# Keys multiplied in place, and K and V loaded in 48 KB runs instead of 24 KB

## The chip, the cores and the metric

One core of one Trainium2 chip. The metric is the device time of one execution in microseconds (us). The kernel before takes 186.91 us (median of 4 runs, 186.84 to 186.94). All comparisons use runs that were recorded as fast; where a run was recorded as slow, it is named and left out. The profiled span is about 1.3 us shorter than the device time. A load of K or V fetches one contiguous run for each of 128 partitions. In the traces each run is one packet, so a load gives each of the 16 DMA engines 8 packets, and each engine reports separately when its part has landed. "First engine" below is the one that reports first.

## The reference, cut to what matters

One decode step of a transformer block for two sequences (B = 2): a modulated layer norm, attention of one query over the last 1,024 keys of 32 heads with 192 numbers each, and a gated feed-forward part. All tensors are bf16.

```python
q = (h @ wq).reshape(B, 1, 32, 192).transpose(0, 2, 1, 3)
k = k_cache[:, :, Sk - 1024:, :]            # B x 32 x 1024 x 192
v = v_cache[:, :, Sk - 1024:, :]
p = softmax(einsum('bhqd,bhkd->bhqk', q, k) * 192 ** -0.5)
o = einsum('bhqk,bhkd->bhqd', p, v) ... @ wo
```

K and V of both sequences are 50 MB of the 76.9 MB that are read. A score needs one multiplication for each number of K, so there is little work for each byte.

## The kernel before

A partition holds one head and a quarter of its positions: 128 partitions are 32 heads x 4 quarters, and each has 256 positions j. A quarter is contiguous in memory, 96 KB for each partition. An arena of six slots of 24 KB for each partition holds weights and tiles of 64 positions of K or V.

```python
TT = 64                        # positions in a tile
SLOT = TT * Dh                 # 12,288 bf16 = 24 KB
NS = 6
tiles = [("k", 0, t) for t in range(NTL)] + [("v", 0, 0)]
for t in range(NTL):
    tiles += [("k", 1, t)] + ([("v", 0, t + 1)] if t + 1 < NTL else [])
tiles += [("v", 1, t) for t in range(NTL)]
for n, it in enumerate(tiles):
    place[it] = ((n + NS - 1) % NS * SLOT, SLOT)
...
def pump(*consumed):           # issue loads, in order, as far as their slots are free
    queue["done"].update(consumed)
    while queue["next"] < len(items):
        it = items[queue["next"]]
        if not all(x in queue["done"] for x in items[:n] if overlap(x, it)):
            break
        S.dma("sp", k_dma(view(it), source(it)), sem_of[it], writes=keys(it), ...)
...
```

The scores of 16 positions are made in three steps. DVE multiplies keys and q into one of four product buffers (`d_mul`). PE adds 192 products down to 32 by six matmuls with the identity (`p_reduce`). DVE sums the rest for two such groups at once (`c_sum`).

```python
def d_mul(b, t, c):
    pz = c % 4
    lo = c % CPT * JC * Dh
    S.op("dve", tensor_tensor(out=prod[:, pz, :, :], in0=view(("k", b, t), lo, ...), in1=qbc[:, b, :]..., op=mult),
         reads=keys(("k", b, t), lo, JC * Dh) + [("qbc", b)], writes=[("prod", pz)])
def p_reduce(b, c):
    ...  # six matmuls: lhsT=ident_b, rhs=prod[:, pz, :, t * GC:(t + 1) * GC]
         # reads=[("prod", pz), "ident_b"], writes=[bank(pz)]
```

After a sequence's last keys comes the softmax. For each 64 positions of V, DVE then makes a masked copy of the weights (`Em`), and PE multiplies it with V (32 matmuls, "PV"). All loads of K, V and weights are issued by SP on one queue, in the order of `items`.

## Time and profile before

The page, as far as the argument needs it. The first three lines are 40 equal slices of the span: busy tenths of DVE, the granted clock of PE, and the busy share of the 16 DMA engines. Below are the load queue's line, the chain that ended last, three groups of instructions (busy us, mean ns | idle before, and what ended it) and the K and V loads with the time from issue to landing.

```profile
DVE  6114000048697696975593999999965856002311
PEclk9999999997988999879559999999998589995597
DMA  9989999999999999999999999999999999999991
...
q1 hardware_dynamic: 4188, 76.88, 97.3%
...
DVE 41%; DMA 35%; PE 21%; SPq 1%; issue 1%; ACT 1%
...
L510 PE MATMUL ps<-prod,ident_b 128*128 128x512 bf16 x192 | 50.7, 410 | 25.1 <-DVE prod L498 24.8
L498 DVE TENSOR_TENSOR prod<-arena,qbc 128x3072 bf16<-128x3072 bf16 x32 | 54.7, 1750 | 2.7 <-DMA arena<-in_A_k_cache_dram 2.7
...
L517 DVE TENSOR_REDUCE S_sb<-ps 128x32 f32<-128x1024 f32 x16 | 19.5, 1221 | 14.4 <-PE ps L510 14.4
...
arena<-in_A_k_cache_dram SPq DMA_DIRECT2D x8, 3072.0 KB, 32.1
arena<-in_A_v_cache_dram SPq DMA_DIRECT2D x8, 3072.0 KB, 23.8
```

The DMA row stands at 9 from the second slice to the last but one, with a single 8, and the queue is busy 97.3% of the span. DVE is busy 57%. So the loads bound the kernel. The chain says "DVE 41%", and this has to be read with care: the chain goes back from the last load through its issue to the computation that freed its slot, although that load then stood in the queue behind others for most of its time. A K load takes 32.1 us to land and occupies the engines only 7.3 us.

The end of the chain, in order of time (start, us, what), shows the tail. The load in its first line is the last but one of w_down; the last lands at 182.78 us, while PE is at work on what came before:

```profile
156.96 25.44 DMA arena<-in_B_w_down_dram
182.40 0.04 issue
182.44 0.65 PE ps L661 x16
...
183.12 0.34 DVE fin L666
```

### The profile page before, as it was taken

To read this page: it belongs to the slowest core of one execution; us is meant where nothing else is said; L and a number is where in the kernel's file an instruction comes from. 1 tells how busy PE (TensorE), PEld (TensorE's weight loads), DVE (VectorE), ACT (ScalarE), POOL (GpSimd) and SP (SyncE) were. 2 spreads that over 40 slices of the span, in tenths; PEclk is the share of its full clock that TensorE was granted. 3 is DMA by queue.
4 is the path that set the end of the run, shared out by engine and by line. 5 is a ranking of instruction groups with operands and counts; after the bars stand their busy time and mean duration, and the time that the engine had idled before them with its cause. 6 is when DMAs were issued, how large, how long until landed. Compare 5 with 4: busy or idle time off the path is not lost.

```text
span 185.6 us, 2065 instructions
## 1 busy us (share of the span) xinstructions
PE 105.1 (57%) x923; PEld 48.5 (26%) x923; DVE 105.1 (57%) x98; ACT 14.2 (8%) x26; POOL 6.4 (3%) x23
## 2 busy tenths in 40 slices
PE   0015720838638375473299496886962599416572
PEld 0011200223213121121253242423311366315321
DVE  6114000048697696975593999999965856002311
ACT  2022100060000000000100000000101000200610
POOL 8500000000000000000000000000000000000000
PEclk9999999997988999879559999999998589995597
DMA  9989999999999999999999999999999999999991
GB/s 331 440 375 450 461 433 403 434 434 424 424 434 424 434 445 434 422 429 429 426 434 424 424 440 422 424 445 440 429 429 429 441 418 456 398 404 421 408 390 38
DMA packets 4213, 77.01 MB, mean 415 GB/s; under 512 B 491, under 2 KB 621, under 8 KB 1261
## 3 DMA queue, kind: packets, MB, share of 16 engines
q1 hardware_dynamic: 4188, 76.88, 97.3%
q8 instruction: 7, 0.11, 0.2%
q14 instruction: 2, 0.01, 0.0%
q10 hardware_dynamic: 16, 0.01, 0.0%
HBM read 76.88 MB, written 0.00 MB: 414 GB/s over the span
## 4 chain that ended last, share of the span: by engine, by line
DVE 41%; DMA 35%; PE 21%; SPq 1%; issue 1%; ACT 1%
DVE prod L498 23%; DMA arena<-in_A_k_cache_dram 21%; DMA arena<-in_B_w_down_dram 14%; PE ps L510 11%; DVE S_sb L517 10%; PE ps L561 8%; DVE Em L547 6%; SPq L282 1%; DVE negm L527 1%; ACT E_sb L535 1%; PE ps L538 1%; PE ps L531 1%; DVE M L523 0%; PE ps L661 0%; PE ps L525 0%
## 5 line engine op out<-in xcount | busy, mean ns | idle before, releaser
L510 PE MATMUL ps<-prod,ident_b 128*128 128x512 bf16 x192 | 50.7, 410 | 25.1 <-DVE prod L498 24.8
L498 DVE TENSOR_TENSOR prod<-arena,qbc 128x3072 bf16<-128x3072 bf16 x32 | 54.7, 1750 | 2.7 <-DMA arena<-in_A_k_cache_dram 2.7
L510 PEld LDWEIGHTS ps<-prod,ident_b 128*128 128x128 bf16 x192 | 17.8, 104 | 57.4 <-DVE prod L498 37.5
L561 PE MATMUL ps<-arena,Em 128*64 128x384 bf16 x256 | 26.1, 369 | 7.1 <-DVE Em L547 7.1
L517 DVE TENSOR_REDUCE S_sb<-ps 128x32 f32<-128x1024 f32 x16 | 19.5, 1221 | 14.4 <-PE ps L510 14.4
L561 PEld LDWEIGHTS ps<-arena,Em 128*64 128x64 bf16 x256 | 15.7, 124 | 17.0 <-DVE Em L547 9.1
L547 DVE TENSOR_TENSOR Em<-E_sb,maskE 128x2048 bf16<-128x2048 bf16 x8 | 18.2, 2283 | 2.8 <-PE ps L561 2.8
L472 PE MATMUL ps<-arena,hT 128*2 128x512 bf16 x60 | 6.6, 615 | 10.0 <-DMA arena<-in_A_wq_dram 9.0
L482 DVE CAST qrow<-ps 128x512 bf16<-128x512 f32 x1 | 0.7, 692 | 15.7 <-PE ps L472 15.7
L611 PE MATMUL ps<-arena,oT 128*17 128x160 bf16 x192 | 5.0, 276 | 6.2 <-DMA arena<-in_A_wo_dram 6.2
L618 DVE TENSOR_TENSOR lnt<-ps,modR 128x160 f32<-128x160 f32 x1 | 0.3, 325 | 14.1 <-PE ps L611 14.1
L611 PEld LDWEIGHTS ps<-arena,oT 128*17 128x17 bf16 x192 | 4.4, 109 | 6.5 <-DMA arena<-in_A_wo_dram 6.5
L472 PEld LDWEIGHTS ps<-arena,hT 128*2 128x2 bf16 x60 | 1.7, 114 | 14.9 <-DMA arena<-in_A_wq_dram 10.0
L568 ACT ACTIVATE On<-ps,rden 128x384 bf16<-128x384 f32 x2 | 1.2, 581 | 57.0 <-PE ps L561 57.0
L535 ACT ACTIVATE E_sb<-S_sb,nbias 128x256 bf16<-128x256 f32 x2 | 1.0, 507 | 57.9 <-DVE nbias L533 57.9
L391 PE MATMUL ps<-ident_b,crow 2*128 2x2 bf16 x5 | 0.4, 177 | 8.2 <-DMA crow<-in_c_dram 8.2
L404 PE MATMUL ps<-st,selstat 128*128 128x2 f32 x4 | 1.1, 350 | 6.1 <-ACT sqj L400 6.1
L450 PE MATMUL ps<-arena,scT 128*17 128x480 bf16 x40 | 4.3, 596 | 0.3 <-DMA arena<-in_w_mod_dram 0.3
L396 DVE CAST X<-xr 128x160 f32<-128x160 bf16 x1 | 0.2, 244 | 7.4 <-DMA xr<-in_A_x_dram 7.4
L632 PE MATMUL ps<-arena,h2T 128*2 128x384 bf16 x40 | 3.8, 484 | 0.6 <-DMA arena<-in_B_w_up_dram 0.3
L641 DVE TENSOR_TENSOR aR<-ps,gl 128x384 bf16<-128x384 f32 x1 | 0.6, 557 | 4.3 <-PE ps L632 4.3
L458 DVE TENSOR_SCALAR opc<-modR 128x160 f32<-128x160 f32 x2 | 0.5, 244 | 4.3 <-ACT modR L455 4.3
(79 smaller groups left out, 49.1 us busy)
## 6 DMA issues: line engine op xcount, KB each, us to landing
arena<-in_A_k_cache_dram SPq DMA_DIRECT2D x8, 3072.0 KB, 32.1
arena<-in_A_v_cache_dram SPq DMA_DIRECT2D x8, 3072.0 KB, 23.8
arena<-in_w_mod_dram SPq DMA_DIRECT2D x1, 4800.0 KB, 14.1
arena<-in_A_wq_dram SPq DMA_DIRECT2D x1, 4608.0 KB, 32.0
arena<-in_A_wo_dram SPq DMA_DIRECT2D x1, 4480.0 KB, 28.3
arena<-in_A_wq_dram SPq DMA_DIRECT2D x1, 3072.0 KB, 20.6
arena<-in_A_wo_dram SPq DMA_DIRECT2D x1, 2720.0 KB, 17.2
arena<-in_B_w_gate_dram SPq DMA_DIRECT2D x1, 1920.0 KB, 20.4
```

Source lines behind the costliest of these rows:

```text
L282: return lambda e: e.dma_start(dst, src)
L450: last = e.matmul(ps[32 * i:32 * i + RM, half, 0:MH].rearrange("p (m n) -> p m n", n=DR), lhsT=scT[:, k, :], rhs=wv[:, 3 * half:3 * half + ...
L472: last = e.matmul(ps[32 * i:32 * i + B, n, :], lhsT=hT[:, k, :], rhs=wv[:, kk, i, n * QW:(n + 1) * QW], start=(k == 0), stop=(k == KT - 1) ...
L498: S.op("dve", lambda e: e.tensor_tensor(out=prod[:, pz, :, :], in0=view(("k", b, t), lo, JC * Dh).rearrange("p (j d) -> p j d", d=Dh), in1 ...
L510: last = e.matmul(o_ap, lhsT=ident_b[:, :], rhs=prod[:, pz, :, t * GC:(t + 1) * GC], start=(t == 0), stop=(t == NCH - 1))
L517: S.op("dve", lambda e: e.tensor_reduce(out=S_sb[:, b, 2 * JC * pair:2 * JC * (pair + 1)], in_=ps[:, 2 * z:2 * z + 2, :].rearrange("p k (j ...
L527: S.op("dve", lambda e: e.tensor_reduce(out=negm[:, b, :].rearrange("p (h x) -> p h x", x=XQ), in_=ps[0:1, BK_T, 0:P].rearrange("p (h x) - ...
L535: S.op("act", lambda e: e.activation(out=E_sb[:, b, :], in_=S_sb[:, b, :], func=ACTF.Exp, scale=SCALE, bias=nbias[:, b:b + 1], accum_out=d ...
L547: S.op("dve", lambda e, z=z, j0=j0: e.tensor_tensor(out=Em[:, z, :, :], in0=E_sb[:, b, j0:j0 + JE].unsqueeze(2).broadcast_to([P, JE, H]), ...
L561: last = e.matmul(ps[64 * i:64 * i + 2 * H, BK_O, 0:ON], lhsT=Em[:, z, 2 * jp:2 * jp + 2, :].rearrange("p j h -> p (j h)"), rhs=view(("v", ...
L611: last = e.matmul(ps[32 * i:32 * i + RM, BK_M, 0:DR], lhsT=oT[:, t, :], rhs=wv[:, tl, i, :], start=(t == 0), stop=(t == NT - 1), tile_posi ...
L632: last = e.matmul(ps[32 * i:32 * i + B, bk, 0:FT].rearrange("p (m r) -> p m r", r=FR), lhsT=h2T[:, k, :], rhs=wk[:, i, :, :], start=(k == ...
```

## The change

The intent is to have the same bytes moved in fewer, longer packets. The products go into the keys' own place, so the four product buffers (24 KB for each partition) become a seventh slot. K and V are loaded in tiles of 128 positions, a run of 48 KB for each partition, except sequence 0's first two K tiles. A K slot now comes free when PE has reduced the products, not when DVE has multiplied. Sums are no longer flushed at the end of each K tile, only where V follows.

```diff
-    NS = 6
+    NS = 7
...
+    K_SPLIT = [[(0, 64), (64, 64), (128, 128)], [(0, 128), (128, 128)]]
+    V_SPLIT = [[(0, 128), (128, 128)], [(0, 128), (128, 128)]]
...
-        for n, it in enumerate(tiles):
-            place[it] = ((n + NS - 1) % NS * SLOT, SLOT)
+        tiles = [("k", 0, 0, 5), ("k", 0, 1, 6), ("k", 0, 2, 0), ("v", 0, 0, 2), ("k", 1, 0, 4), ("v", 0, 1, 0), ("k", 1, 1, 2), ("v", 1, 0, 4), ("v", 1, 1, 0)]
+        for kind, b, t, z in tiles:
+            j0, n = (K_SPLIT if kind == "k" else V_SPLIT)[b][t]
+            place[(kind, b, t)] = (z * SLOT, n * Dh)
...
-        prod = sb("prod", [P, 4, JC, Dh], BF16)
...
-            S.op("dve", lambda e: e.tensor_tensor(out=prod[:, pz, :, :], in0=view(("k", b, t), lo, JC * Dh)..., op=ALU.mult),
-                 reads=keys(("k", b, t), lo, JC * Dh) + [("qbc", b)], writes=[("prod", pz)], ...)
+            S.op("dve", lambda e: e.tensor_tensor(out=kt, in0=kt, in1=qbc[:, b, :]..., op=ALU.mult),
+                 reads=[("qbc", b)], writes=keys(it, lo, JC * Dh), ...)
...
-                    last = e.matmul(o_ap, lhsT=ident_b[:, :], rhs=prod[:, pz, :, t * GC:(t + 1) * GC], ...)
+                    last = e.matmul(o_ap, lhsT=ident_b[:, :], rhs=kt[:, :, t * GC:(t + 1) * GC], ...)
...
-            c_sum(b, (t + 1) * CPT // 2 - 1)
+            if nxt[0] == "v":
+                c_sum(b, (j0 + w) // JC // 2 - 1)
```

The weights' places follow (w_o in slots 2, 3 and 6, the feed-forward weights in slots 4 and 5). The order of the items is as before except for the larger tiles.

More of the change, by code (lines that the diff above doesn't have):

```diff
@@ L161, in bass_adaLN_cond__sliding_block_cached__geglu_ffn__decode_kernel @@
     ON = 2 * Dh
-    TT = 64
     JE = 64
-    NTL = J // TT
-    CPT = TT // JC
-    SLOT = TT * Dh
+    SLOT = JE * Dh
     UNIT = 128
-    assert NTL * TT == J and CPT % 2 == 0 and TT % JE == 0
+    K_SPLIT = [[(0, 64), (64, 64), (128, 128)], [(0, 128), (128, 128)]]
+    V_SPLIT = [[(0, 128), (128, 128)], [(0, 128), (128, 128)]]
+    assert all(sum(n for _, n in x) == J and all(n % JE == 0 for _, n in x) for x in K_SPLIT + V_SPLIT)
     WQ_SPLIT = [(0, 2), (2, 3)]
@@ L194, in bass_adaLN_cond__sliding_block_cached__geglu_ffn__decode_kernel @@
         place = {("wm", 0): (0, KT * 6 * D), ("wq", 0): (2 * SLOT, wq_n[0]), ("wq", 1): (2 * SLOT + wq_n[0], wq_n[1])}
-        tiles = [("k", 0, t) for t in range(NTL)] + [("v", 0, 0)]
-        for t in range(NTL):
-            tiles += [("k", 1, t)] + ([("v", 0, t + 1)] if t + 1 < NTL else [])
-        tiles += [("v", 1, t) for t in range(NTL)]
-        for n, it in enumerate(tiles):
-            place[it] = ((n + NS - 1) % NS * SLOT, SLOT)
-        for i, (t0, _) in enumerate(WO_SPLIT):
-            place[("wo", i)] = (3 * SLOT + t0 * D, wo_n[i])
-        o_g, o_u = 0, KT * F
+        tiles = [("k", 0, 0, 5), ("k", 0, 1, 6), ("k", 0, 2, 0), ("v", 0, 0, 2), ("k", 1, 0, 4), ("v", 0, 1, 0), ("k", 1, 1, 2), ("v", 1, 0, 4), ("v", 1, 1, 0)]
+        span = {}
+        for kind, b, t, z in tiles:
+            j0, n = (K_SPLIT if kind == "k" else V_SPLIT)[b][t]
+            place[(kind, b, t)] = (z * SLOT, n * Dh)
+            span[(kind, b, t)] = (j0, n)
+        tiles = [it[:3] for it in tiles]
+        place[("wo", 0)] = (2 * SLOT, wo_n[0])
+        place[("wo", 1)] = (6 * SLOT, wo_n[1])
+        place[("wo", 2)] = (2 * SLOT + wo_n[0], wo_n[2])
+        o_g = 4 * SLOT
+        o_u = o_g + KT * F
         o_d = o_u + KT * F
@@ L209, in bass_adaLN_cond__sliding_block_cached__geglu_ffn__decode_kernel @@
             place[("wd", i)] = (o_d + r0 * D, nr * D)
-        assert len(tiles) == 16 and wq_n[0] + wq_n[1] <= 3 * SLOT
         assert all(o % UNIT == 0 and n % UNIT == 0 and o + n <= NAR for o, n in place.values())
@@ L320, in source @@
                 return B_w_down.rearrange("(p r) n -> p (r n)", r=FC)[:, r0 * D:(r0 + nr) * D]
-            _, b, t = it
+            b, (j0, n) = it[1], span[it]
             src = A_k_cache if kind == "k" else A_v_cache
-            return src[b][:, K0:Sk, :].rearrange("h (x j) d -> h x j d", x=XQ)[:, :, t * TT:(t + 1) * TT, :].rearrange("h x j d -> h x (j d)")
+            return src[b][:, K0:Sk, :].rearrange("h (x j) d -> h x j d", x=XQ)[:, :, j0:j0 + n, :].rearrange("h x j d -> h x (j d)")
         def pump(*consumed):
@@ L493, in bass_adaLN_cond__sliding_block_cached__geglu_ffn__decode_kernel, with d_mul, p_reduce @@
                  reads=[bank(BK_T + b)], writes=[("qbc", b)], name="q2_evac%d" % b)
-        def d_mul(b, t, c):
-            pz = c % 4
-            lo = c % CPT * JC * Dh
-            S.op("dve", lambda e: e.tensor_tensor(out=prod[:, pz, :, :],
-                                                  in0=view(("k", b, t), lo, JC * Dh).rearrange("p (j d) -> p j d", d=Dh),
-                                                  in1=qbc[:, b, :].unsqueeze(1).broadcast_to([P, JC, Dh]), op=ALU.mult),
-                 reads=keys(("k", b, t), lo, JC * Dh) + [("qbc", b)], writes=[("prod", pz)], name="mul%d_%d" % (b, c))
-        def p_reduce(b, c):
-            pz = c % 4
+        def d_mul(it, c):
+            b, lo = it[1], (c * JC - span[it][0]) * Dh
+            kt = view(it, lo, JC * Dh).rearrange("p (j d) -> p j d", d=Dh)
+            S.op("dve", lambda e: e.tensor_tensor(out=kt, in0=kt, in1=qbc[:, b, :].unsqueeze(1).broadcast_to([P, JC, Dh]), op=ALU.mult),
+                 reads=[("qbc", b)], writes=keys(it, lo, JC * Dh), name="mul%d_%d" % (b, c))
+        def p_reduce(it, c):
+            b, lo = it[1], (c * JC - span[it][0]) * Dh
+            pz = c % 4
+            kt = view(it, lo, JC * Dh).rearrange("p (j d) -> p j d", d=Dh)
             def f(e):
@@ L509, in f @@
                 for t in range(NCH):
-                    last = e.matmul(o_ap, lhsT=ident_b[:, :], rhs=prod[:, pz, :, t * GC:(t + 1) * GC],
+                    last = e.matmul(o_ap, lhsT=ident_b[:, :], rhs=kt[:, :, t * GC:(t + 1) * GC],
                                     start=(t == 0), stop=(t == NCH - 1))
                 return last
-            S.op("pe", f, reads=[("prod", pz), "ident_b"], writes=[bank(pz)], name="red%d_%d" % (b, c))
+            S.op("pe", f, reads=keys(it, lo, JC * Dh) + ["ident_b"], writes=[bank(pz)], name="red%d_%d" % (b, c))
         def c_sum(b, pair):
@@ L541, in softmax, with weights_v, p_pv, f @@
                  reads=[bank(BK_T)], writes=[("rden", b)], name="rec_%d" % b)
-        def weights_v(b, t):
-            for s in range(TT // JE):
-                z = (t * (TT // JE) + s) % 2
-                j0 = t * TT + s * JE
-                S.op("dve", lambda e, z=z, j0=j0: e.tensor_tensor(out=Em[:, z, :, :], in0=E_sb[:, b, j0:j0 + JE].unsqueeze(2).broadcast_to([P, JE, H]),
-                                                                  in1=maskE[:, :].unsqueeze(1).broadcast_to([P, JE, H]), op=ALU.mult),
-                     reads=[("E", b), "maskE"], writes=[("Em", z)], name="Em%d_%d" % (b, j0))
-        def p_pv(b, t):
-            for s in range(TT // JE):
-                z = (t * (TT // JE) + s) % 2
-                j0 = t * TT + s * JE
-                lo = s * JE * Dh
-                def f(e, z=z, j0=j0, lo=lo):
+        def weights_v(it):
+            b, (j0, n) = it[1], span[it]
+            for j in range(j0, j0 + n, JE):
+                z = j // JE % 2
+                S.op("dve", lambda e, z=z, j=j: e.tensor_tensor(out=Em[:, z, :, :], in0=E_sb[:, b, j:j + JE].unsqueeze(2).broadcast_to([P, JE, H]),
+                                                                in1=maskE[:, :].unsqueeze(1).broadcast_to([P, JE, H]), op=ALU.mult),
+                     reads=[("E", b), "maskE"], writes=[("Em", z)], name="Em%d_%d" % (b, j))
+        def p_pv(it):
+            b, (j0, n) = it[1], span[it]
+            for j in range(j0, j0 + n, JE):
+                z = j // JE % 2
+                lo = (j - j0) * Dh
+                def f(e, z=z, j=j, lo=lo):
                     last = None
@@ L562, in f @@
                                         lhsT=Em[:, z, 2 * jp:2 * jp + 2, :].rearrange("p j h -> p (j h)"),
-                                        rhs=view(("v", b, t), lo + 2 * jp * Dh, ON),
-                                        start=(j0 == 0 and jp < 2), stop=(j0 == J - JE and jp >= JE // 2 - 2), tile_position=(0, 64 * i))
-                    return last
-                S.op("pe", f, reads=[("Em", z)] + keys(("v", b, t), lo, JE * Dh), writes=[bank(BK_O)], name="PV%d_%d" % (b, j0))
-            if t == NTL - 1:
+                                        rhs=view(it, lo + 2 * jp * Dh, ON),
@@ L568, in p_pv @@
+                                        start=(j == 0 and jp < 2), stop=(j == J - JE and jp >= JE // 2 - 2), tile_position=(0, 64 * i))
+                    return last
+                S.op("pe", f, reads=[("Em", z)] + keys(it, lo, JE * Dh), writes=[bank(BK_O)], name="PV%d_%d" % (b, j))
+            if j0 + n == J:
                 S.op("act", lambda e: e.activation(out=On[:, b, :], in_=ps[:, BK_O, 0:ON], func=ACTF.Identity, scale=rden[:, b:b + 1]),
                      reads=[bank(BK_O), ("rden", b)], writes=[("On", b)], name="On_%d" % b)
-        for n, (kind, b, t) in enumerate(tiles):
+        made = set()
@@ L572, in bass_adaLN_cond__sliding_block_cached__geglu_ffn__decode_kernel @@
+        for n, it in enumerate(tiles):
+            kind, b, t = it
             nxt = tiles[n + 1] if n + 1 < len(tiles) else None
             if kind == "v":
-                if n == 0 or tiles[n - 1][0] == "v" or (b, t) == (tiles[n - 1][1], 0):
-                    weights_v(b, t)
-                p_pv(b, t)
-                pump((kind, b, t))
+                if it not in made:
+                    weights_v(it)
+                p_pv(it)
+                pump(it)
                 continue
-            for c in range(t * CPT, (t + 1) * CPT):
-                d_mul(b, t, c)
-                p_reduce(b, c)
-                if c % 2 == 0 and c > t * CPT:
-                    c_sum(b, c // 2 - 1)
@@ L584, in bass_adaLN_cond__sliding_block_cached__geglu_ffn__decode_kernel @@
-            pump((kind, b, t))
-            if nxt and nxt[0] == "v" and nxt[1] != b:
-                weights_v(nxt[1], nxt[2])
-            c_sum(b, (t + 1) * CPT // 2 - 1)
-            if t == NTL - 1:
+            j0, w = span[it]
+            last = j0 + w == J
+            for c in range(j0 // JC, (j0 + w) // JC):
+                d_mul(it, c)
+                p_reduce(it, c)
+                if c % 2 == 0 and c > 0 and ("S", b, c // 2 - 1) not in made:
+                    c_sum(b, c // 2 - 1)
@@ L589, in bass_adaLN_cond__sliding_block_cached__geglu_ffn__decode_kernel @@
+            pump(it)
+            if nxt[0] == "v" and nxt[1] != b:
+                weights_v(nxt)
+                made.add(nxt)
+            if nxt[0] == "v":
+                c_sum(b, (j0 + w) // JC // 2 - 1)
+                made.add(("S", b, (j0 + w) // JC // 2 - 1))
+            if last:
                 softmax(b)
```

## The prediction

> What bounds the kernel now. Data transfer, from end to end. The page gives the loads' queue 97.3% of sixteen engines' span, and the slices of DMA share stay at nine tenths from the second to the last. The windows view gives a DMA share of 0.99 to 1.02 in every 12 us stretch from 38 to 172 us. The 24 KB K tiles take 32.1 us from issue to landing, though one occupies the engines only 7.3 us, so some four are always queued. The chain of waits starts on a K load and ends on the last w_down load (landing 182.4 us), then 0.65 us PE, two 0.3 us DVE steps and the store.
>
> What the change does to the transfers. The bytes are the same. Packet records: a 24,576 B packet takes 914 ns (median), a 36,864 B one 1,364, a 38,400 B one 1,420. That is 0.0366 ns per byte plus about 14 ns per packet. A 49,152 B packet should then take about 1,814 ns (estimate), against 1,828 for two of 24 KB. Seven pairs of tiles become 48 KB runs: per engine 7 x 8 = 56 packets fewer, 56 x 14 = 0.78 us, and seven 9 ns semaphore writes fewer: 0.85 us in all, all on the bounding resource. The Trainium skill, "DMA: Bandwidth & Descriptors", section "Why small descriptors are slow", gives a fixed overhead per packet; the trace agrees, and shows it is nearly spent at 24 KB.
>
> What it does to the engines. The multiply (1.68 us, 32 of them) writes over its input; I expect the same time. Four product buffers go, and the sums are no longer flushed at each K tile's end, where DVE waited about 1.5 us for PE (at 49.7 and 61.4 us). All of this is off the critical path.
>
> The risk. A K slot comes free only after PE's reduction, not after the multiply, and frees come in 48 KB lumps. Stepping the new order with the trace's durations (multiply 1.68, sum 1.15, Em 2.2, reduction 1.48, PV block 2.8, softmax 3.8 us; 1.3 us from free to first byte), the slot is free before the queue runs dry by roughly: V0 second half 5 to 6 us, K1 second half 1.5 to 8, V1 first half -0.5 to 6, V1 second half 8 to 14, first w_o 6 to 7. Before, the worst such margin was 2 us. The low ends are PE at half clock in the first PV (5.33 us a block, as at 92.7 us). "TensorE: Matmul & The Clock Gate", Part 1, says the clock halves after an idle window of about 3.4 us; the trace agrees (half clock after the softmax, 88.0 to 98.3 us). PV now ends at about 158 to 163 us, still before the last w_o lands at 168.
>
> Sum: 186.9 - 0.85 = 186.05 without a stall; about one chance in four of a stall of 0.5 to 2 us. Predicted 186.2 us, 185.5 to 187.5.
>
> Faster by over 2%: 0.01. Within 2%: 0.96. Slower: 0.03.
>
> What shows each step: 49,152 B packets near 1,814 ns; no dip in DMA share near 104 or 118 us; last load landing near 181.9 us; multiplies still 1.68 us; fewer DVE waits on PE before 85 us; V1's first load issued before about 117 us.
>
> What would make it wrong: 48 KB packets slower per byte; in-place multiplies slower; half clock during K1 emptying the queue; a stall at V1's first load.

## More of the kernel before

SP's issues in time (start, us to the end of the last of the row) show how far ahead loads are issued:

```profile
83.89 0.54 SPq L282 DMA_DIRECT2D arena<-in_A_k_cache_dram  x1
98.07 0.54 SPq L282 DMA_DIRECT2D arena<-in_A_v_cache_dram  x1
103.81 0.54 SPq L282 DMA_DIRECT2D arena<-in_A_k_cache_dram  x1
108.87 17.75 SPq L282 DMA_DIRECT2D arena<-in_A_v_cache_dram  x4
```

The load at 98.07 us is the last quarter of V of sequence 0. The load in front of it lands at 104.68 us on the DMA engine that is done first, so this issue, the tightest of the K and V stage, is 6.6 us ahead.

## The result, and the profile after

| | before | after |
|---|---|---|
| device time, median of 4 runs | 186.91 us | 186.29 us |
| range | 186.84 to 186.94 | 186.01 to 186.47 |
| data packets of the load queue, each engine | 232.5 | 176.5 |
| last wq load lands to last V load lands, first DMA engine | 116.87 us | 116.35 us |
| last w_down load landed | 182.78 us | 182.12 us |
| multiply, mean | 1,750 ns | 1,749 ns |

The ratio is 0.9966, 95% interval 0.9949 to 0.9983: 0.3% less time, clear of noise, and well inside 2%. A ratio here and below is the mean time of one kernel's fast runs over that of the other's fast runs of the same rounds, so it is not quite the ratio of the medians. Executions over 1.5% slower than the fastest of the same kernel are left out of the means.

The lines of the page after that answer to those shown of before:

```profile
DVE  6113000039994589965994999287995658102311
PEclk9999995559999759997599999987999569996576
DMA  9989999999898989999898989999898999899991
...
q1 hardware_dynamic: 3180, 76.88, 97.2%
...
DMA 57%; DVE 22%; PE 17%; ACT 1%; issue 1%; SPq 1%
...
L510 PE MATMUL ps<-arena,ident_b 128*128 128x512 bf16 x192 | 50.0, 404 | 29.2 <-DVE arena L498 29.2
L498 DVE TENSOR_TENSOR arena<-arena,qbc 128x3072 bf16<-128x3072 bf16 x32 | 54.7, 1749 | 11.5 <-DMA arena<-in_A_k_cache_dram 11.5
...
L517 DVE TENSOR_REDUCE S_sb<-ps 128x32 f32<-128x1024 f32 x16 | 19.5, 1218 | 7.5 <-PE ps L510 7.5
...
arena<-in_A_v_cache_dram SPq DMA_DIRECT2D x4, 6144.0 KB, 27.1
arena<-in_A_k_cache_dram SPq DMA_DIRECT2D x3, 6144.0 KB, 41.5
```

The queue has 1,008 packets fewer: 896 of data (56 for each engine) and 112 of the 4 bytes by which a load reports its end. The 8s in the DMA row are no gaps: the row books a packet where it starts, and packets now last as long as 0.4 of a slice. Counted packet by packet, all 16 engines were at work in every 4 us from 16 to 176 us, before and after.

DVE's wait for PE's reductions fell from 14.4 to 7.5 us, as the unflushed sums promise. In its place DVE waits 8.8 us longer for keys. That is the cost of large tiles, which can be used only when all of them have landed. Neither matters for the time, for the loads are the bound. The chain says so too: its DVE share halves and the time moves by a third of a percent.

The tail is nearly the same: 0.74 us of PE (0.65 before) from the landing of the last load but one, two DVE steps and the store. The last load lands at 182.12 us.

```profile
155.92 25.81 DMA arena<-in_B_w_down_dram
181.73 0.04 issue
181.78 0.74 PE ps L668 x16
...
182.54 0.34 DVE fin L673
```

SP's issues after, and so the lead of the tightest one:

```profile
82.83 0.54 SPq L282 DMA_DIRECT2D arena<-in_A_v_cache_dram  x1
96.75 0.54 SPq L282 DMA_DIRECT2D arena<-in_A_k_cache_dram  x1
112.83 6.66 SPq L282 DMA_DIRECT2D arena<-in_A_v_cache_dram  x2
136.02 2.00 SPq L282 DMA_DIRECT2D arena<-in_A_wo_dram  x3
```

The first load at 112.83 us is V's first half of sequence 1. The load in front of it lands at 118.81 us on the first engine, so it is issued 6.0 us ahead, against 6.6 for the tightest one before.

The packet records of the trace (these are counts and medians over the records of the two profiled runs, not lines of a view):

```
packet      before                 after
24,576 B    2,176 of 914 ns        384 of 912 ns
49,152 B    -                      896 of 1,820 ns (mean 1,821)
35,840 B    128 of 1,329 ns        128 of 1,329 ns
```

### The profile page after: what moved, and what is told of

Its sections match the earlier page's. It is cut to its first block, busy times and chain, and to the rows that moved or that the text cites. A ratio compares the mean times of both kernels' runs of the same rounds, so it can differ in the third digit from the quotient of the medians.

```text
span 185.0 us, 2053 instructions
## 1 busy us (share of the span) xinstructions
PE 103.4 (56%) x923; PEld 47.5 (26%) x923; DVE 104.9 (57%) x98; ACT 14.2 (8%) x26; POOL 6.4 (3%) x23
## 4 chain that ended last, share of the span: by engine, by line
DMA 57%; DVE 22%; PE 17%; ACT 1%; issue 1%; SPq 1%
DMA arena<-in_A_k_cache_dram 36%; DMA arena<-in_B_w_down_dram 14%; DVE arena L498 12%; DMA arena<-in_w_mod_dram 8%; PE ps L561 7%; DVE S_sb L517 6%; PE ps L510 5%; DVE Em L547 2%; PE ps L450 2%; DVE negm L527 1%; ACT E_sb L535 1%; SPq L282 1%; PE ps L538 1%; DVE M L523 0%; PE ps L531 0%
## 5 line engine op out<-in xcount | busy, mean ns | idle before, releaser
L510 PE MATMUL ps<-arena,ident_b 128*128 128x512 bf16 x192 | 50.0, 404 | 29.2 <-DVE arena L498 29.2
L498 DVE TENSOR_TENSOR arena<-arena,qbc 128x3072 bf16<-128x3072 bf16 x32 | 54.7, 1749 | 11.5 <-DMA arena<-in_A_k_cache_dram 11.5
L510 PEld LDWEIGHTS ps<-arena,ident_b 128*128 128x128 bf16 x192 | 17.3, 102 | 61.5 <-DVE arena L498 42.9
L561 PE MATMUL ps<-arena,Em 128*64 128x384 bf16 x256 | 24.4, 356 | 5.6 <-DVE Em L547 5.6
L618 PE MATMUL ps<-arena,oT 128*17 128x160 bf16 x192 | 4.2, 250 | 4.0 <-DMA arena<-in_A_wo_dram 3.2
L618 PEld LDWEIGHTS ps<-arena,oT 128*17 128x17 bf16 x192 | 3.7, 97 | 4.3 <-DMA arena<-in_A_wo_dram 3.4
L488 PE MATMUL ps<-qrow,selq 128*128 128x192 bf16 x16 | 2.7, 364 | 1.2 <-ACT qrow L479 1.2
```

The lines of the kernel that those rows point to most:

```text
L488: last = e.matmul(ps[:, BK_T + b, 0:Dh], lhsT=selq[:, b, u * P:(u + 1) * P], rhs=qrow[:, u * Dh:(u + 1) * Dh], start=(u == 0), stop=(u == ...
L498: S.op("dve", lambda e: e.tensor_tensor(out=kt, in0=kt, in1=qbc[:, b, :].unsqueeze(1).broadcast_to([P, JC, Dh]), op=ALU.mult), reads=[("qb ...
L510: last = e.matmul(o_ap, lhsT=ident_b[:, :], rhs=kt[:, :, t * GC:(t + 1) * GC], start=(t == 0), stop=(t == NCH - 1))
L561: last = e.matmul(ps[64 * i:64 * i + 2 * H, BK_O, 0:ON], lhsT=Em[:, z, 2 * jp:2 * jp + 2, :].rearrange("p j h -> p (j h)"), rhs=view(it, l ...
L618: last = e.matmul(ps[32 * i:32 * i + RM, BK_M, 0:DR], lhsT=oT[:, t, :], rhs=wv[:, tl, i, :], start=(t == 0), stop=(t == NT - 1), tile_posi ...
```

## The experiments

The theory: the kernel is bound by its loads, every packet costs a DMA engine some 10 ns beyond its bytes, and the gain is the 56 packets fewer. The edits are shown shortened. The rivals: the gain comes from the engines (in-place products, fewer waits, other slots), or from fewer loads and completions, or is chance.

### The changed kernel again

No edit. 5 rounds, on the same chip and in the same rounds as the next three.

> Control: the changed kernel as it is. Theory (fewer, longer packets in a load-bound kernel): again 186.0 to 186.5 us, 0.3 to 0.4% under the kernel before. Rival (a chance difference of the four runs): no clear difference from 186.9.

Measured: 186.41 us (186.29 to 186.59), ratio 0.9974, interval 0.9961 to 0.9986. The gain is not chance. Its interval overlaps that of the first four runs, so the two sizes are not told apart.

### The same slots, but two loads of 24 KB for each run

```diff
-    queue["ops"][it] = S.dma("sp", k_dma(view(it), source(it)), sem_of[it], writes=keys(it), ...)
+    for lo, w in pieces(it):        # K and V in pieces of PIECE = 12288 elements
+        queue["ops"][it] = S.dma("sp", k_dma(view(it, lo, w), source(it)[..., lo:lo + w]), sem_of[(it, lo)], writes=keys(it, lo, w), ...)
```

> The changed kernel, slots, order and in-place products kept, but each 48 KB run is fetched by two loads of 24 KB. Packet theory: the gain is lost. 56 packet pairs per engine cost 11 ns more each (two of 916 ns against one of 1,821 ns), 0.62 us, and seven semaphore packets of 9 ns: 186.9 to 187.0 us, last w_down load landing about 182.8 us. Rival (the gain comes from the engines: in-place products, fewer waits of DVE for PE, the new slots): stays at 186.3.

Measured: 186.91 us (186.88 to 187.03), ratio 1.0002, interval 0.9989 to 1.0014. The whole gain is gone, with seven slots, in-place products and the new order still there. Last load landed at 182.82 us (before: 182.78). The stage from the last wq load to the last V load takes 116.88 us on the first engine, as before (116.87).

### Pieces of 12 KB

The same edit with `PIECE = 6144`.

> As a24, with pieces of 12 KB: a second dose. Packet theory: a 12,288 B packet, by a straight line between 9,216 B (350 ns) and 15,360 B (578 ns), takes about 464 ns; four take 1,858 against 1,821: 56 x 37 ns = 2.1 us, 0.3 us more for the two 24 KB tiles of K0, 0.2 us of semaphore packets. About 188.9 us, 188.3 to 189.5. Rival (engines): 186.3.

Measured: 188.23 us (188.03 to 188.40), ratio 1.0069, interval 1.0057 to 1.0082. Direction as the theory says, size below my range. The packets took 464 ns as estimated, but the stage took 118.17 us, only 1.30 us more than with 24 KB, for 128 packets more on each engine: 10.1 ns for each. From 48 to 24 KB it was 0.52 us for 56: 9.3 ns. Both include the completions. Two doses at nearly the same price fit a fixed cost for each packet; that longer runs are read better for another reason is not excluded. The estimate failed because I added up the durations of packet records, and records of neighbouring packets of one engine overlap by a few ns. The 0.2 us for completions did not show either. The distance from landing to landing is what counts: 7.305 us for eight packets of 24 KB (913.1 ns each, although a record says 916 on average), 14.535 us for eight of 48 KB (1,816.9 ns, record 1,821), and 3.69 us for eight of 12 KB (462 ns, record 464).

### The kernel before with products in place, nothing else

```diff
-            S.op("dve", lambda e: e.tensor_tensor(out=prod[:, pz, :, :], in0=view(("k", b, t), lo, JC * Dh)..., ...),
-                 reads=keys(("k", b, t), lo, JC * Dh) + [("qbc", b)], writes=[("prod", pz)], ...)
+            S.op("dve", lambda e: e.tensor_tensor(out=kt, in0=kt, ...),
+                 reads=[("qbc", b)], writes=keys(("k", b, t), lo, JC * Dh), ...)
```

> The kernel before, with only the products written over the keys (six slots and 24 KB loads kept; a K slot comes free after PE's reduction, about 1.5 us later). Packet theory: 186.9 us as before, multiplies still 1.75 us. Rival (in-place products bring the gain): 186.3. If in-place products cost something: multiplies longer than 1.75 us.

Measured: 186.96 us (186.79 to 187.09), ratio 1.0001, interval 0.9988 to 1.0015. In-place products neither cost nor gain anything by themselves; the multiplies' line:

```profile
L497 DVE TENSOR_TENSOR arena<-arena,qbc 128x3072 bf16<-128x3072 bf16 x32 | 54.7, 1749 | 2.6 <-DMA arena<-in_A_k_cache_dram 2.6
```

### As many packets, twice the loads

Each 48 KB tile is fetched by two loads of every second partition. The packets stay at 48 KB; loads and completions double.

```diff
+    for g in (0, 1):
+        S.dma("sp", k_dma(view(it)[g:P:2, :], source(it)[:, g:XQ:2, :]), sem_of[(it, g)], writes=keys(it, halves=(g,)), ...)
```

> The changed kernel with each 48 KB run tile fetched by two loads of 64 partitions each (every second partition): twice the loads and completions of those tiles, but as many packets, still of 48 KB. Packet theory: 186.4 us, at most 0.1 us more (seven more loads, 9 ns a semaphore packet), 49,152 B packets still near 1,820 ns. Rival (the number of loads and their completions is what counts, not the packets): 186.9 us, as with two 24 KB loads. Open: if 64 partitions are served worse by the engines, the packets would be longer and the run says nothing.

Measured: 186.44 us (186.32 to 186.55), ratio 0.9969, interval 0.9956 to 0.9982. The page shows that it did what it should. It has 112 packets more than the changed kernel, all of them 4-byte completions (seven loads x 16 engines), and still the stage took 116.35 us.

```profile
q1 hardware_dynamic: 3292, 76.88, 97.1%
...
arena<-in_A_k_cache_dram SPq DMA_DIRECT2D x8, 3072.0 KB, 36.8
```

So the number of loads is not it. The number of packets is, or, what these runs cannot separate from it, their length.

### How near is an empty queue? Extra DVE work

After sequence 0's softmax, DVE makes the first `Em` again, once or four times (EXTRA is 1 or 4). The result stays right.

```diff
-            for j in range(j0, j0 + n, JE):
+            for j in [j0] * (EXTRA if it == ("v", 0, 0) else 0) + list(range(j0, j0 + n, JE)):
```

> The changed kernel with one Em step (2.28 us of DVE) done twice after batch 0's softmax. Theory (engines off the critical path; in the trace V1's first half is issued at 112.8 us, about 1.3 us before its first byte can move, and the queue runs dry at about 118.3: 4.2 us of margin, 5.7 at K1's second half): no change, 186.4 us, within 0.2. Rival (DVE time counts): 188.7 us.

Measured: 186.36 us (186.26 to 186.42), ratio 0.9965, interval 0.9953 to 0.9977. 2.3 us of DVE work in the middle of the kernel cost nothing.

> The same step done four more times, 9.1 us of DVE. Theory: the margin of 4.2 us before V1's first half is used up and 4 to 6 us of empty queue appear there (K1's second half late by 9.1 - 5.7 = 3.4 us first): 190 to 192 us, with a dip of the DMA share between 103 and 125 us. Rival A (all DVE time counts): 195.5 us. Rival B (slots have nothing to do with it): 186.4 us.

Measured: 192.28 us (191.64 to 193.33), ratio 1.0288, interval 1.0261 to 1.0314. Of 9.1 us, some 5.9 reach the time. The windows (busy us of each engine, then PE clock, DMA share, GB/s) show the two gaps that the theory asked for:

```profile
90.00:100.00 10.00, 0.57 (x4) 0.37 (x6) 9.86 (x6) 0.00 (x0) 0.00 (x0) 0.50 0.94 408
100.00:110.00 10.00, 10.00 (x79) 5.57 (x76) 7.42 (x5) 0.00 (x0) 0.00 (x0) 0.86 0.61 241
110.00:120.00 10.00, 6.29 (x26) 2.02 (x24) 10.00 (x8) 0.00 (x0) 0.00 (x0) 1.00 1.09 472
120.00:130.00 10.00, 8.23 (x77) 4.65 (x78) 10.00 (x7) 0.58 (x1) 0.00 (x0) 1.00 0.84 331
```

```profile
106.46 0.54 SPq L282 DMA_DIRECT2D arena<-in_A_k_cache_dram  x1
122.54 6.66 SPq L282 DMA_DIRECT2D arena<-in_A_v_cache_dram  x2
```

The load before the one at 106.46 had landed at 104.38 us. The first new packet starts 1.3 us after the issue began, and the first packet then takes 2,284 to 2,660 ns on 14 of the engines (1,832 and 2,095 on the two that start last) instead of 1,820. The landing that follows is 18.73 us after the one before, not 14.53: 4.20 us lost. The second gap costs 1.61 us (16.14 us between landings). Together they make 5.8 us.

### The same extra work in the kernel before

The same edit on the kernel before, four times.

> The kernel before with the same Em step done four more times after batch 0's softmax (9.1 us of DVE). Theory: its margin is as thin as that of the changed one: V0's last quarter was issued at 98.1 us, its packets start at 104.2, and a load must be issued some 3 us ahead; so 9.1 - 3.1 = about 5 to 6 us of loss in ONE gap, for slots then come free every 7 us: 191.5 to 192.8 us. The changed kernel lost 5.9 us in two gaps. Rival (the change made the schedule more fragile than it was): under 190 us here.

Measured: 188.72 and 189.75 us in the two fast runs; two more, 192.04 and 193.41, were recorded as slow and are left out. Ratio 1.0124, interval 1.0095 to 1.0153. On these two runs the verdict goes to the rival: the kernel before loses 2.3 us (their mean, against 186.9) where the changed one loses 5.9. But the two runs left out are called slow for their time alone; their granted clocks (0.879 and 0.889) lie within those of the other two (0.875 and 0.900). With all four the loss would be 4.1 us, so how much more fragile the change made the schedule stays open. My expectation of one gap was right (landings 10.00 us apart instead of 7.30, so 2.70 us lost), but the gap was smaller than I thought, for in this run the load was issued at 105.04 us, only 7.0 us later than in the plain kernel's trace. With two runs the size is loosely known.

```profile
105.04 0.53 SPq L282 DMA_DIRECT2D arena<-in_A_v_cache_dram  x1
110.66 0.54 SPq L282 DMA_DIRECT2D arena<-in_A_k_cache_dram  x1
```

After one late load the kernel before is in time again with the next, 5.6 us later. In the changed kernel a slot pair comes free once per 48 KB tile, and the next load was late as well.

### More of the change: all K in 48 KB, and w_q in one run of 60 KB

```diff
-    K_SPLIT = [[(0, 64), (64, 64), (128, 128)], ...
+    K_SPLIT = [[(0, 128), (128, 128)], ...
-    WQ_SPLIT = [(0, 2), (2, 3)]
+    WQ_SPLIT = [(0, 5)]
```

> More of the change: batch 0's keys also in two 48 KB runs, and w_q in one run of 60 KB instead of 24 and 36. 16 packets per engine fewer than the changed kernel, at 9 to 10 ns each 0.15 us: about 186.25 us if no slot comes free too late; the first multiply starts about 7 us later (48 us). Rival (late start of the multiplies delays the end): 187 us or more, and V0's second half issued after 89 us.

Measured: 187.05 to 189.27 us in four fast runs (two more, 189.86 and 189.94, slow); ratio 1.0052, interval 1.0016 to 1.0087. Fewer packets, and slower than both kernels. In the trace the first multiply starts at 47.86 us instead of 40.65, and then:

```profile
85.15 0.54 SPq L282 DMA_DIRECT2D arena<-in_A_v_cache_dram  x1
99.86 0.54 SPq L282 DMA_DIRECT2D arena<-in_A_k_cache_dram  x1
115.94 6.66 SPq L282 DMA_DIRECT2D arena<-in_A_v_cache_dram  x2
```

So the rival's outcome came, but not at the place that it named: V's second half of sequence 0 was in time (85.15, not after 89), V's first half of sequence 1 was not. It was issued 2.8 us before the load in front of it landed on the first engine. That engine lost 0.27 us. Packets right after took up to 3,449 ns, and the last w_down load landed at 183.24 us, 1.1 us later than in the changed kernel's trace. The late load explains little of this: the first engine landed its last load only 0.15 us later than in the changed kernel (180.35 against 180.20 us), and 15 of the 16 were done at 182.19 us (182.12 there for all). The one that ended 1.05 us behind them was in line with the others until 178.7 us. A 16 KB packet of instructions runs at 179.36 us, and the packets that follow it, of 6,400 and 3,840 bytes, take 681 and 269 ns instead of 248 and 149. So in this trace some 1 us of the loss is an instruction packet on an engine that was among the last. Whether the other runs (187.05 to 189.94 us) lost their time at the late load I can't show, as only this one has a trace.

### Only w_q in one run

> The changed kernel with only w_q in one run of 60 KB (one of the two things that the run with all K in 48 KB did). If that run's loss came from w_q, the time is again 187 us or more. If it came from the late first multiply (47.9 instead of 40 us), as its trace suggests (V1's first half issued at 115.9 us, packets of 2,000 to 3,400 ns right after), this one is at 186.3 us, 8 packets per engine at about 9 ns under the changed kernel's 186.4, too little to tell; the first multiply at 40 to 41 us, V1's first half issued at 112 to 114 us.

Measured: 186.23 us (186.10 to 186.44), ratio 0.9966, interval 0.9952 to 0.9979. So w_q in one run does no harm by itself, and the loss of the run before came with the K tiles, the other thing that it changed. Their late first multiply is the likely path, but its trace shows only 0.27 us of it. Here the first multiply is on time:

```profile
40.69 5.10 DVE L498 TENSOR_TENSOR arena<-arena,qbc 128x3072 bf16<-128x3072 bf16 x3 [1.71 <-ACT qbc L492]
```

This version beats the kernel before. Against the changed kernel's 186.29 and 186.41 us it is not told apart.

### The lead that a load needs

Seven issues side by side. "Lead" is how long before the landing of the load in front of it (first engine) a load was issued, and "lost" how much later than the undisturbed distance its own landing came.

```
kernel, load                         lead us   lost us
changed, V1 first half                 5.98      0.0
w_q in one run, V1 first half          4.64      0.0
one extra Em, V1 first half            3.67      0.0
all K in 48 KB, V1 first half          2.76      0.27
four extra Em, V1 first half           0.57      1.61
four extra Em, K1 second half         -2.08      4.20
kernel before, four extra, V0 last    -0.49      2.70
```

In the last three rows lead and loss add up to 2.1 or 2.2 us. A load issued that late leaves its engines empty; at 2.8 us it was still disturbed, at 3.7 no longer. So the changed kernel has 2.3 to 3.8 us to spare at its tightest load, worked out as 5.98 less 3.67 or 2.2.

## Why the prediction was right

The prediction was 186.2 us, 185.5 to 187.5; measured 186.29, and 186.41 in the second set. Point by point:

- **Loads bound the kernel throughout.** Right. 2.3 us of extra DVE work cost nothing, and 56 or 128 packets more on each engine showed in the time.
- **The gain is the packets, 0.85 us.** The step is right and shown by undoing it alone: with 24 KB pieces the gain is gone, with twice the loads and as many packets it stays. The size was too large. "About 14 ns per packet", the intercept of a line through packet durations, was the term mis-sized: the stage shows 9.3 ns for each packet saved, completions included, so 0.52 us. The medians differ by 0.62 us in the first set and 0.50 in the second. A 48 KB packet took 1,820 ns, not 1,814. That 186.2 lies so near 186.29 is in part luck: it holds 0.15 us for a stall that did not come, against a gain put 0.33 us too high for the stage. The Trainium skill, "DMA: Bandwidth & Descriptors", section "Why small descriptors are slow", names a fixed overhead for each packet; the runs agree, with 9.3 ns between 48 and 24 KB and 10.1 ns between 24 and 12 KB. That these ns are the overhead that the page means is not shown.
- **The 9 ns completions count.** Wrong, as far as the runs show: seven loads more left the stage at 116.35 us, where seven times 9 ns would make 0.06 us.
- **Engines off the critical path.** Right: in-place products alone gave ratio 1.0001, and the new slots and order with 24 KB loads 1.0002. Multiplies kept their time.
- **Fewer DVE waits for PE.** Right (14.4 to 7.5 us), and worth nothing here, as said.
- **The margins.** With the prediction's own rule (1.3 us from free to first byte) the trace gives about 5 us at V0's second half, 5.7 at K1's second half, 4.2 at V1's first half and 10 at w_o. The first three lie in the ranges given; w_o had more room than the 6 to 7 said. No stall came. Two things were wrong beside that. The worst margin before was put at 2 us; its lead of 6.6 us shows more room than in the changed kernel. And 1.3 us is not all that a load needs: with the slower first packets it is 2.1 to 2.2, and it was disturbed at 2.8.
- **The clock.** "TensorE: Matmul & The Clock Gate", Part 1, has the clock halve after idle windows. The changed kernel's trace agrees: half clock from 86.0 to 92.8 us, around the softmax, after 3.4 us in which PE had 0.9 us of work, so the window was not quite idle. The first PV still freed its slot in time, and the last PV ended at 159.8 us, before the last w_o load (168.2), as predicted.

## What to carry to other kernels

When one queue of loads is busy from end to end, count packets and bytes for each DMA engine, and cost a packet by the distance from landing to landing, not by its record; here that is 9 to 10 ns of about 913. Room in on-chip memory is then worth having for longer runs even if no computation gets faster. But larger tiles come free in larger lumps: check for each load how long before the landing of its predecessor it can be issued, and stop enlarging before that lead goes under the smallest that was seen undisturbed (3.7 us here; 2.8 was disturbed). One step further, and the kernel was slower than at the start, though the one trace of it puts most of that elsewhere. And look at which DMA engine ends last: a single engine, held up near the end, sets the time.

## What the Trainium skill lacked or had wrong

- "DMA: Bandwidth & Descriptors", section "Why small descriptors are slow", finds it worth combining descriptors into packets only up to 256 bytes. That is not the same as making runs longer, and the section gives no figure for runs of this length. In a kernel bound by its queue, going from 24 to 48 KB gave 9.3 ns for each packet saved, a clear 0.3% of the time.
- The same page, "Latency and other measured facts", gives a first byte after about 600 ns for loads issued by SP. The page does not say from where it counts. In the run with four extra steps the first packet started 1.3 us after its issue began (106.46 to 107.78 us) and 0.8 us after it ended, the first packet of 14 engines took 2,284 to 2,660 ns instead of 1,820, and a load needed a lead of more than 2.8 us for an undisturbed queue. No page that I read gives the lead.
- "Runtime: NRT & Kernel Launch", section "Instruction fetch mechanics", calls the cost of refilling instructions in 16 KiB blocks mostly hidden. In a load-bound kernel it is not hidden from the loads. Each trace has seven instruction packets of 16 KB, of 0.93 to 1.11 us, on the DMA engines. In the changed kernel the one at 76.90 us is followed by a 48 KB packet of 2,322 instead of 1,820 ns. The last load's landings are spread from 180.20 to 182.12 us over the 16 engines; how much of that spread these packets make was not tested. In the trace with all K in 48 KB, one engine ends 1.05 us behind the other 15 after such a packet.
- "HBM Reference", "Specifications (TRN2)", gives about 358 GB/s for a core and says that a core alone measures about 425. Here it was 430 to 434 GB/s from 31 to 149 us.
